# Weight splits on VectorE alone, an earlier register load and regrouped folds in a three-stage fp32 kernel

## The chip, the cores and the metric

The kernel runs on one core of a Trainium2 chip. The metric is the device time of one execution in microseconds (us). Engines are called PE (TensorE), DVE (VectorE), ACT (ScalarE), POOL (GpSimd) and SP (SyncE, which only issues transfers here); PEld is the weight load of TensorE.

## The reference

Three stages are chained: a linear attention with decay over chunks, a mixture of eight experts with one expert for each token, and an FNet block (a Fourier transform over sequence and channels, then a two-layer network). All data are fp32.

```python
# attention: x (4,8,768,32), a (4,8,768), B and C (4,8,768,16), chunks of 32
L = exp(cum[:, None] - cum[None, :]) * causal          # cum: cumulated log a of the chunk
y = (C @ B.T * L) @ x + (C @ state) * exp(cum)
state = exp(sum(la)) * state + B.T @ (x * exp(cum[-1] - cum))
# experts: x (4,768,256), w1 (8,256,1024), w2 (8,1024,256)
fresh = argmax(x @ w_gate)
e = fresh if s == 0 or sigmoid(x @ w_local) < 0.5 else previous token's e
out = p[e] * (relu(x @ w1[e]) @ w2[e])
# FNet
u = x + real(fft(fft(x, axis=1), axis=2))
out = u + relu(layernorm(u) @ w_ch1) @ w_ch2
```

## The kernel before

**Products.** Every fp32 operand of the large products is split into a high part h, rounded to the type fp32r, and a low part l = value - h. One product is then three: hh, hl and lh. The high part of a weight is made by ACT (L180, 128x1024 at a time), the low part by a subtraction of two operands in SBUF (L185): of each 1024 columns VectorE takes the first 384 and GpSimd the other 640. A weight matrix (w1 or w2 of an expert) has two such halves, called q = 0 and 1. SP loads the raw matrices (L160 w1, L164 w2) into a ring of two buffers, which the raw weights of the last network (`rawc`, L115 and L121) share; a buffer is free again when both engines have finished the low part that reads it.

**Stage one** (`phase_a`, from L221): 6 chunks of 128 positions by 2 pairs of batches make 12 passes (`for i, (c, bp) in enumerate(pairs)`). In a pass PE makes small products (g at L414, yb at L445, tl at L498), which are masked by VectorE (mt, L422), and GpSimd prepares operands (ce L338, xt L400, sn L477). Between them a generator, `routing` (from L504), decides the expert of each token by some twenty short VectorE steps for a chunk (mx, kd, ls, cand, ff, er, ot, ac, exo, sx, px, ro, rk, si), interleaved by `gap`, `place` and `leave`. GpSimd then scatters the tokens by row number into xs_buf in HBM (L617). When the last are out, the 256 first tokens of expert 0 are read back (xe, L623). The first expert's split is called from the passes: w1 in passes 8 and 9, the high part of w2 in 9 and 10 and behind them; its low part comes at the start of stage two. `warm` (L262) and `keep_clock` (L213) are products without use that keep PE going.

**Stage two.** `ffn` (L829) runs one expert's tokens: eight column blocks of the first layer (mm1: six products at L839 each, into a ring of three PSUM buffers; then ACT's relu hh, L843, and VectorE's hl, L844), then for each 128 tokens 24 products of the second layer (L851), ACT's y (L900) and GpSimd's scatter into y_tok (L901). Expert 0 comes in two parts, 256 early tokens and 256 others; the seven others run in an order by count (`order`, L793) with 512 tokens for four of them and 384 for the last three. After each mm1 block (0 to 7) and each 128 tokens (8 and on) a hook runs, which sets the order of the rest: the split of the next expert's w1 at hooks 1 and 4, of its w2 at 9 and 10; the tokens of the next expert (xn, loaded by SP at L879) are transposed at hook 7 (tp, L863); `prep_wch` splits pieces of the last network's weights (VectorE L130 to L133, GpSimd L139 and L140). At the end `overflow` (L910) computes on VectorE how many more rounds of experts are needed, loads that number into a register of all five engines (L924) and branches on it (L927); no more are needed with these inputs.

**Stage three** takes z from y_tok (SP, L1026) and runs six groups of 512 rows. For a batch, two `fold` generators (part 0 is a sum, part 1 a difference) make r from z: eo (L1056), tp (L1062), tm (L1065), sp, and r (L1069 to L1074). Two of the six r blocks are on GpSimd (L1069, L1070), and so are eo and tp of part 1 of the first batches. PE transforms r (`stage_a`, L1110, f), corrects and goes on (L1124 and on); VectorE and GpSimd add rows to u (L1157). `run(b, p, n)` takes n steps of fold p of batch b; the order of the opening is written out by hand as such calls.

Of the kernel before, what the change touches and what calls it, by code (L numbers as in the profile page):

```python
# [11 lines left out]
ALU = mybir.AluOpType  # L12
# [5 lines left out]
NE, F = 8, 1024  # L18
# [32 lines left out]
def tile_kernel(ctx: ExitStack, tc: tile.TileContext, io):  # L51
# [103 lines left out]
    def load_w(e, part=None, static=False):  # L155
# [11 lines left out]
        def pieces():  # L167
            out = []
            for k, n, sh in ((0, "w1", [128, 2, F]), (1, "w2", [128, 8, D])):
                r = raws.pop((e, k))  # L170
                hi = wsp.tile(sh, FP32R, tag=n + "h", name=n + "h")
                lo = wsp.tile(sh, FP32R, tag=n + "l", name=n + "l")
                out += [hi, lo]
                h = hi.rearrange("p k f -> p (k f)")
                l_ = lo.rearrange("p k f -> p (k f)")
                r_ = r.rearrange("p k f -> p (k f)")
                ahead = e == 0 and k == 1 and not static

                def high(q):
                    A.activation(out=h[:, q * F:q * F + F], in_=r_[:, q * F:q * F + F], func=ACTF.Copy)  # L180

                def low(q, engs):
                    for eng, x, y in engs:
                        x, y = q * F + x, q * F + y
                        eng.tensor_tensor(out=l_[:, x:y], in0=r_[:, x:y], in1=h[:, x:y], op=ALU.subtract)  # L185

                v, g = (V, 0, 384), (G, 384, F)
                if ahead:
                    for q in range(2):
                        high(q)  # L190
                        yield
                    for eng in (g, v):
                        for q in range(2):
                            low(q, (eng,))
                        if eng is g:
                            yield
                else:
                    for q in range(2):
                        high(q)
                        low(q, (v, g))  # L200
                        if q == 0:
                            yield
                if len(out) == 4:
                    wt[e] = out
                yield
# [15 lines left out]
    def phase_a():  # L221
        with ExitStack() as st:
# [434 lines left out]
            def leave(late=1):  # L657

                if scq and now[0] >= scq[0][2] + late:
                    f, bb, _ = scq.pop(0)  # L660
                    f(bb)
# [28 lines left out]
            for i, (c, bp) in enumerate(pairs):  # L690
# [77 lines left out]
                gap(6)  # L768
                if i in (8, 9, 10):
                    next(ws)  # L770
                    route["ws"] = ws

            g2 = pg.tile([128, 2, 2, 128], FP32, tag="g2", name="g2")[:].rearrange("p u h i -> p (u h i)")
            while rq:
                for r in sorted(rq, key=lambda q: q[2]):
                    if r[1][1]():
                        on = r[1][0]
                        step(r)
                        if on == "p":
                            warm(1, 512, g2)  # L780
                leave(0)
            while scq:
                leave(0)
            next(ws)
            cps = pg.tile([128, 2, 2, 128], FP32, tag="g0", name="cps")[:, 0, 0, 0:NE + 1]
# [123 lines left out]

    def overflow(pools):  # L910

        sm = pools[3]
        ex = sm.tile([128, NE], FP32, tag="oex", name="oex")
        for n in set(CAPS):
# [8 lines left out]
        V.tensor_scalar(out=ri, in0=mx[:, 0:1], scalar1=1.0 / CAP, scalar2=1.499, op0=ALU.mult, op1=ALU.add)  # L923
        nr = nc.values_load(  # L924
            ri[0:1, 0:1], min_val=1, max_val=NTOK // CAP + 1, skip_runtime_bounds_check_because="counts lie in 1..3072"
        )
        with tc.If(nr > 1):  # L927
            ro = sm.tile([128, 4], FP32, tag="oro", name="oro")
# [22 lines left out]
    with ExitStack() as st:  # L951
# [8 lines left out]
        with tc.manual_schedule():  # L960
# [3 lines left out]
            for _ in ws:  # L964
                pass
            nxt, od = None, order(sm)

# [13 lines left out]
            for e in range(NE):  # L981
# [4 lines left out]
                def hook(i):  # L986
                    nonlocal nxt, ws
                    at = (1, 4, 9, 10) if e else (1, 3, 8, 9)
# [13 lines left out]
                wt.pop(e)  # L1002
        overflow((xp, hp, yp, sm, ps1, ps2, pst))
    if "dbg_y" in dbg:
# [4 lines left out]
    with ExitStack() as st:  # L1009
# [35 lines left out]
        def fold(b, part, e1, e2):  # L1045
# [22 lines left out]
            yield  # L1068
            G.tensor_tensor(out=r[:, 3, :], in0=tm[:, 1, :], in1=tm[:, 2, :], op=ALU.add)  # L1069
            G.tensor_tensor(out=r[:, 5, :], in0=tp[:, 1, :], in1=tp[:, 2, :], op=ALU.subtract)  # L1070
            e2.tensor_tensor(out=r[:, 0, :], in0=tp[:, 0, :], in1=sp[:, 0, :], op=ALU.add)
# [161 lines left out]
        with tc.manual_schedule():  # L1233
# [7 lines left out]
            def run(b, p, n=1):  # L1241
                f = fm.get((b, p))
                if f is None:
                    f = fm[b, p] = mid(b) if p == 2 else fold(b, p, G if b > 1 or p else V, V)
                for _ in range(n):
                    next(f)

            run(0, 0)
            run(0, 1)
            run(0, 0, 2)  # L1250
            run(0, 1, 2)
            load_k(0)
            run(1, 0)
            run(1, 1)
            stage_a(0, 0)
# [22 lines left out]
            load_k(1)  # L1278
            run(1, 1)

# [129 lines left out]
```

## Time and profile before

| | us |
|---|---|
| median of 3 runs | 471.1 |
| lowest and highest run | 470.17, 471.72 |
| the profiled execution's own time | 467.85 |
| its span on the core | 466.1 |
| PE busy in the span | 429.4 |
| DVE busy | 272.7 |
| POOL busy | 205.5 |
| ACT busy | 187.1 |

The mean granted clock of PE in the profiled execution is 0.985 of full speed. Busy shares are means over three stages that have different limits. A row of the timeline has the start in us, the duration, the engine, the line, the operation with its output and input, the count, and in brackets how long the engine had been idle and what ended that. The program's names are shared by many instructions, so that mm, say, is the output of L839 and of L851.

### The profile page before, as it was taken

The page shows a single profiled execution, that of the slowest core. Times are in us where ns is not written, and L with a number is a line of the kernel's source. Part 1 is how long each engine was busy: PE and PEld are TensorE (multiplying, and loading weights), DVE is VectorE, ACT ScalarE, POOL GpSimd, SP SyncE. Part 2 cuts the span into 40 slices and gives each one's busy share as a digit, 9 for nine tenths or more (in the row PEclk, how much of TensorE's full clock was granted, in tenths as well). Part 3 has the DMA queues.
Part 4 walks back from the last instruction along what each step waited for, and adds up shares of the span by engine and source line. Part 5 has one row for each costly group of instructions (what it writes and reads, how often), then busy time and mean ns, then how long its engine had stood idle before and what let it go on. Part 6 is the DMA issues. An engine that isn't in the chain of part 4 may idle for free.

```text
span 466.1 us, 8953 instructions
## 1 busy us (share of the span) xinstructions
PE 429.4 (92%) x3429; PEld 370.2 (79%) x3429; DVE 272.7 (59%) x708; ACT 187.1 (40%) x400; POOL 205.5 (44%) x231
## 2 busy tenths in 40 slices
PE   8798788868999899999889879989999999999997
PEld 4576565468989798989879863669989899998986
DVE  5677878584456636464574624786555578564241
ACT  2455463234555445555453411353341443333130
POOL 2237785354437383839493644835302261400000
PEclk9999998999999999999999997999999999999999
DMA  8899411227253645354545116200231100010101
GB/s 277 263 329 350 167 48 49 70 80 242 99 184 124 189 126 186 125 172 133 172 175 169 66 35 227 90 23 1 72 110 51 65 23 25 2 45 1 45 1 45
DMA packets 32891, 54.26 MB, mean 116 GB/s; under 512 B 3301, under 2 KB 22149, under 8 KB 32840
## 3 DMA queue, kind: packets, MB, share of 16 engines
q1 hardware_dynamic: 29400, 45.86, 30.0%
q0 software_dynamic: 2928, 7.46, 4.6%
q8 instruction: 29, 0.48, 0.5%
q10 hardware_dynamic: 512, 0.28, 0.2%
q14 instruction: 22, 0.18, 0.1%
HBM read 41.63 MB, written 12.61 MB: 116 GB/s over the span
## 4 chain that ended last, share of the span: by engine, by line
PE 73%; DVE 12%; DMA 5%; ACT 5%; issue 3%; POOL 1%; SPq 0%; POOLq 0%; ACTq 0%; DVEq 0%
PE mm L851 30%; PE mm L839 26%; DMA xn<-xs_buf 3%; PE tl L498 3%; PE tp L863 2%; PE g L414 2%; PE f L1110 2%; DVE mt L422 2%; PE mb L262 2%; DVE w1l L185 2%; PE yb L445 1%; ACT x1t L452 1%; PE cps L1124 1%; DMA y_tok<-y,ids 1%; DMA z<-y_tok 1%
## 5 line engine op out<-in xcount | busy, mean ns | idle before, releaser
L844 DVE SCALAR_TENSOR_TENSOR hl<-mm,hh 128x512 fp32r<-128x512 f32 (+2 forms) x120 | 74.4, 626 | 59.3 <-ACT hh L843 59.0
L843 ACT ACTIVATE hh<-mm 128x512 fp32r<-128x512 f32 (+2 forms) x120 | 65.1, 547 | 89.1 <-PE mm L839 89.1
L851 PE MATMUL mm<-w2h,hh 128*128 128x256 f32 x232 | 64.9, 280 | 0.0
L851 PE MATMUL mm<-w2l,hh 128*128 128x256 f32 x232 | 64.2, 277 | 0.0
L851 PE MATMUL mm<-w2h,hl 128*128 128x256 f32 x232 | 64.2, 277 | 0.0
L839 PE MATMUL mm<-xh,w1h 128*128 128x512 f32 (+2 forms) x144 | 51.0, 359 | 8.9 <-DVE hl L844 8.3
L851 PE MATMUL mm<-c2h,hh 128*128 128x256 f32 x192 | 54.4, 283 | 0.0
L851 PE MATMUL mm<-c2h,hl 128*128 128x256 f32 x192 | 53.8, 280 | 0.0
L851 PE MATMUL mm<-c2l,hh 128*128 128x256 f32 x192 | 53.7, 280 | 0.0
L901 POOL DMA_INDIRECT y_tok<-y,ids x27 | 28.8, 1068 | 48.7 <-ACT y L900 45.8
L839 PE MATMUL mm<-xh,w1l 128*128 128x512 f32 (+2 forms) x144 | 50.2, 353 | 0.0
L851 PEld LDWEIGHTS mm<-w2h,hl 128*128 128x128 f32 x232 | 43.7, 188 | 0.0
L851 PEld LDWEIGHTS mm<-w2h,hh 128*128 128x128 f32 x232 | 43.6, 188 | 0.0
L851 PEld LDWEIGHTS mm<-w2l,hh 128*128 128x128 f32 x232 | 43.6, 188 | 0.0
L839 PE MATMUL mm<-xh,c1h 128*128 128x512 f32 x96 | 39.5, 411 | 0.6 <-ACT xh L865 0.6
L839 PE MATMUL mm<-xl,w1h 128*128 128x512 f32 (+2 forms) x144 | 39.0, 351 | 0.0
L839 PEld LDWEIGHTS mm<-xh,w1h 128*128 128x128 f32 x144 | 27.6, 192 | 13.2 <-DVE hl L844 10.1
L839 PE MATMUL mm<-xh,c1l 128*128 128x512 f32 x96 | 37.9, 395 | 0.0
L851 PEld LDWEIGHTS mm<-c2l,hh 128*128 128x128 f32 x192 | 36.1, 188 | 0.1
L851 PEld LDWEIGHTS mm<-c2h,hh 128*128 128x128 f32 x192 | 36.1, 188 | 0.1
L851 PEld LDWEIGHTS mm<-c2h,hl 128*128 128x128 f32 x192 | 36.1, 188 | 0.0
L185 POOL TENSOR_TENSOR w1l<-r,w1h 128x640 fp32r<-128x640 f32 x16 | 28.5, 1780 | 15.4 <-ACT w1h L180 15.4
(331 smaller groups left out, 897.2 us busy)
## 6 DMA issues: line engine op xcount, KB each, us to landing
r<-in_w_dram SPq DMA_DIRECT2D x16, 1024.0 KB, 9.3
rawc<-in_wc_dram SPq DMA_DIRECT2D x8, 512.0 KB
out_dram<-o SPq DMA_DIRECT2D x24, 128.0 KB, 1.7
z<-y_tok SPq DMA_DIRECT2D x3, 768.0 KB
xs_buf<-scr SPq DMA_DIRECT2D x8, 265.0 KB, 7.5
xn<-xs_buf SPq DMA_DIRECT2D x4, 530.0 KB, 6.5
c1h<-in_x_dram SPq DMA_DIRECT2D x4, 512.0 KB, 5.6
xk<-y_tok SPq DMA_DIRECT2D x4, 512.0 KB, 3.8
```

The source lines that it names most:

```text
L185: eng.tensor_tensor(out=l_[:, x:y], in0=r_[:, x:y], in1=h[:, x:y], op=ALU.subtract)
L262: PE.matmul(out=ps[:, 0:w], lhsT=wrm[:, 0:128], rhs=wrm[:, 0:w], start=True, stop=True)
L414: PE.matmul(out=gp[q][:, u].rearrange("p h i -> p (h i)"), lhsT=lds[c]["bt"][r:r + 32, 2 * bp + u, :], rhs=ch[r:r + 32, u].rearrange("p q ...
L422: V.tensor_tensor(out=m[:, :, 2 * q:2 * q + 2, :], in0=gp[q], in1=cc("cmask").unsqueeze(1).unsqueeze(1).to_broadcast([128, 2, 2, 128]), op ...
L498: PE.matmul(out=tl[:, 128 * g:128 * g + 137], lhsT=x1t[:, g, u, :], rhs=ca[:, o:o + 137], start=(g == 0), stop=(g == 1), skip_group_check= ...
L839: PE.matmul(out=ps[:, 0:n], lhsT=w[:, d, f * 128:(f + 1) * 128], rhs=x[:, d, 0:n], start=(k == 0), stop=(k == 5))
L843: A.activation(out=hf, in_=ps[:, 0:n], func=ACTF.Relu)
L844: V.scalar_tensor_tensor(out=hl[:, f, 0:n], in0=ps[:, 0:n], scalar=0.0, in1=hf, op0=ALU.max, op1=ALU.subtract)
L851: PE.matmul(out=ps, lhsT=h[:, f, t * 128:(t + 1) * 128], rhs=w[:, f, :], start=(k == 0), stop=(k == 23))
L863: PE.transpose(ps[d][:, t * 128:(t + 1) * 128], src(t, d), ident)
L901: w = G.indirect_dma_start(out=y_tok, out_offset=bass.IndirectOffsetOnAxis(ap=ids[:, t:t + 1], axis=0), in_=y, in_offset=None, bounds_chec ...
L1110: PE.matmul(out=ps[:, k2, :], lhsT=r[:, zi, :], rhs=fa[:, ci, :], start=(i == 0), stop=(i == len(terms) - 1),)
```

## The change

There are three edits.

**Splits.** The low part of every weight is made by VectorE alone, 128x1024 for a half. For the first expert a half is two pieces of 128x512, and the calls come earlier: in passes 7 to 10 one each, in pass 10 a second one; then one behind each product step of the routing's tail, until four more have been taken.

**Rounds.** The number of extra rounds is computed at hook 2 of expert 1 by a generator `rounds` and loaded into the registers at hook 8 of that expert; `overflow` takes the register and only branches.

**Folds.** Of batch 0 all steps of both folds are on VectorE, part 0 ahead of part 1. The first step of the second fold of batch 1 (GpSimd, eo 128x768) moves from ahead of `stage_a(0, 0)` to behind `load_k(1)`.

```diff
-                v, g = (V, 0, 384), (G, 384, F)
-                if ahead:
+                if ahead and k:
                     for q in range(2):
                         high(q)
                         yield
-                    for eng in (g, v):
-                        for q in range(2):
-                            low(q, (eng,))
-                        if eng is g:
-                            yield
-                else:
-                    for q in range(2):
+                for q in range(2):
+                    if not (ahead and k):
                         high(q)
-                        low(q, (v, g))
-                        if q == 0:
-                            yield
+                    if ahead:
+                        low(q * F, q * F + F // 2)
+                        yield
+                        low(q * F + F // 2, q * F + F)
+                    else:
+                        low(q * F, q * F + F)
+                    if q == 0:
+                        yield
...
-                if i in (8, 9, 10):
+                if 7 <= i < NP - 1:
                     next(ws)
+                    if i == 10:
+                        next(ws)
...
                         if on == "p":
                             warm(1, 512, g2)
+                            if low[0] < 4:
+                                next(ws)
+                                low[0] += 1
...
+                    if (e, i) == (1, 2):
+                        nr = rounds(sm)
+                        next(nr)
+                    if (e, i) == (1, 8):
+                        nr = next(nr)
...
-            G.tensor_tensor(out=r[:, 3, :], in0=tm[:, 1, :], in1=tm[:, 2, :], op=ALU.add)
-            G.tensor_tensor(out=r[:, 5, :], in0=tp[:, 1, :], in1=tp[:, 2, :], op=ALU.subtract)
+            e3 = G if b else V
+            e3.tensor_tensor(out=r[:, 3, :], in0=tm[:, 1, :], in1=tm[:, 2, :], op=ALU.add)
+            e3.tensor_tensor(out=r[:, 5, :], in0=tp[:, 1, :], in1=tp[:, 2, :], op=ALU.subtract)
...
-                    f = fm[b, p] = mid(b) if p == 2 else fold(b, p, G if b > 1 or p else V, V)
+                    f = fm[b, p] = mid(b) if p == 2 else fold(b, p, G if b > 1 or b and p else V, V)
...
-            run(0, 0)
-            run(0, 1)
-            run(0, 0, 2)
-            run(0, 1, 2)
+            run(0, 0, 3)
+            run(0, 1, 3)
             load_k(0)
             run(1, 0)
-            run(1, 1)
             stage_a(0, 0)
...
             load_k(1)
-            run(1, 1)
+            run(1, 1, 2)
```

What stood on VectorE in the routing's tail, where exo to si are the last steps ahead of the scatters of the last tokens:

```order
L587 TENSOR_TENSOR exo<-ex,ot 128x16
L591 TENSOR_REDUCE sx<-ex 128x2
L551 SCALAR_TENSOR_TENSOR er<-kr 2x128
L593 TENSOR_SCALAR sx<-sx 128x2
L595 RECIPROCAL sx<-sx 128x2
L567 TENSOR_TENSOR ot<-cb,f__1417 128x2x8
```

The same place in the changed kernel, where L183 is the low part:

```order
L584 TENSOR_TENSOR exo<-ex,ot 128x16
L183 TENSOR_TENSOR w2l<-r_914,w2h 128x512 x2
L588 TENSOR_REDUCE sx<-ex 128x2
L548 SCALAR_TENSOR_TENSOR er<-kr 2x128
L590 TENSOR_SCALAR sx<-sx 128x2
L183 TENSOR_TENSOR w2l<-r_914,w2h 128x512
L592 RECIPROCAL sx<-sx 128x2
L564 TENSOR_TENSOR ot<-cb,f__1419 128x2x8
```

Three pieces of w2's low part now stand between steps of the routing; a fourth follows some rows later. Before, they came after the whole tail.

GpSimd in the middle of stage two, from one 512-token expert to the next:

```order
L185 TENSOR_TENSOR w1l<-r_2595,w1h 128x640 x2
L901 DMA y_tok<-y,ids 3072x256
L139 TENSOR_TENSOR ce__2762<-cv,c1h 128x512
L140 TENSOR_TENSOR c1l<-ce__2762,cr 128x512
L901 DMA y_tok<-y,ids 3072x256
L185 TENSOR_TENSOR w2l<-r_2597,w2h 128x640
L901 DMA y_tok<-y,ids 3072x256
```

And now, where L906 is the scatter:

```order
L906 DMA y_tok<-y,ids 3072x256 x4
L139 TENSOR_TENSOR ce__2518<-cv,c1h 128x512
L140 TENSOR_TENSOR c1l<-ce__2518,cr 128x512
L906 DMA y_tok<-y,ids 3072x256 x4
L139 TENSOR_TENSOR ce__2761<-cv,c1h 128x512
```

Scatters and the two steps of `prep_wch` are left; four subtractions an expert went to VectorE.

GpSimd at the opening of stage three, from the folds of batch 0 to the first rows u:

```order
L1062 TENSOR_TENSOR tp__5527<-eo 128x384
L1069 TENSOR_TENSOR r_5517<-tm__5520 128x128
L1070 TENSOR_TENSOR r_5517<-tp__5519 128x128
L1069 TENSOR_TENSOR r_5525<-tm__5528 128x128
L1070 TENSOR_TENSOR r_5525<-tp__5527 128x128
L1039 DMA xk<-y_tok,rix 128x256 x2
L1056 TENSOR_TENSOR eo<-z 128x768
L1157 TENSOR_TENSOR u<-xk,a 128x256
```

And now, where L1053 loads xk, L1172 makes u and L1070 is eo:

```order
L1053 DMA xk<-y_tok,rix 128x256 x2
L1172 TENSOR_TENSOR u<-xk,a 128x256
L1173 TENSOR_TENSOR u<-xk,a 128x1
L1172 TENSOR_TENSOR u<-xk,a 128x256
L1173 TENSOR_TENSOR u<-xk,a 128x1
L1172 TENSOR_TENSOR u<-xk,a 128x256
L1173 TENSOR_TENSOR u<-xk,a 128x1
L1084 TENSOR_TENSOR r_5495<-tm__5498 128x128
L1085 TENSOR_TENSOR r_5495<-tp__5497 128x128
...
L1053 DMA xk<-y_tok,rix 128x256 x2
L1070 TENSOR_TENSOR eo<-z 128x768
```

The rows u are the first thing that GpSimd does in the stage; eo of batch 1's second fold comes behind the second xk.

## Rows read from the trace of the kernel before

**Rows 1.** From the page: busy time by engine; the chain that ended last.

```profile
PE 429.4 (92%) x3429; PEld 370.2 (79%) x3429; DVE 272.7 (59%) x708; ACT 187.1 (40%) x400; POOL 205.5 (44%) x231
...
PE 73%; DVE 12%; DMA 5%; ACT 5%; issue 3%; POOL 1%; SPq 0%; POOLq 0%; ACTq 0%; DVEq 0%
```

**Rows 2.** Timeline of PE, rows behind a wait: start, us, what, [idle before <-releaser].

```profile
70.47 1.38 PE L414 MATMUL g<-ch,c2h 32*128 32x256 f32 x4 [0.91 <-DVE mt L422]
72.02 2.52 PE L414 MATMUL g<-ch,c2h 32*128 32x256 f32 x12 [0.17 <-DVE mt L422]
...
101.62 0.39 PE L839 MATMUL mm<-xh,w1h 128*128 128x256 f32 x1 [3.28 <-DVE hl L844]
...
115.28 0.39 PE L839 MATMUL mm<-xh,w1h 128*128 128x256 f32 x1 [1.65 <-DVE hl L844]
...
159.79 1.07 PE L863 MATMUL tp<-ca,xn 128*128 128x128 f32 x8 [1.78 <-DMA xn<-xs_buf]
...
226.68 0.85 PE L863 MATMUL tp<-ca,xn 128*128 128x128 f32 x6 [1.43 <-DMA xn<-xs_buf]
...
243.37 0.63 PE L839 MATMUL mm<-xh,w1h 128*128 128x384 f32 x1 [2.05 <-DVE hl L844]
...
264.81 0.44 PE L839 MATMUL mm<-xh,w1h 128*128 128x384 f32 x1 [1.30 <-DVE hl L844]
...
279.08 2.93 PE L213 MATMUL wps<-fa 128*128 128x512 f32 x3 [3.44 <-ACTq L927]
...
294.18 1.16 PE L1110 MATMUL f<-fa,r 128*128 128x128 f32 x8 [0.89 <-POOL r L1069]
...
305.62 0.51 PE L839 MATMUL mm<-xh,c1h 128*128 128x512 f32 x1 [0.58 <-ACT xh L865]
```

**Rows 3.** Timeline of DVE: short mask steps, low parts, and the first fold.

```profile
33.40 0.21 DVE L587 TENSOR_TENSOR exo<-ex,ot 128x32 f32<-128x32 f32 x1
...
66.00 0.56 DVE L185 TENSOR_TENSOR w1l<-r,w1h 128x384 fp32r<-128x384 f32 x1 [1.42 <-ACT w1h L180]
66.48 3.33 DVE L587 TENSOR_TENSOR exo<-ex,ot 128x32 f32<-128x32 f32 x1
...
97.46 3.77 DVE L812 TENSOR_TENSOR bg<-at,cb 128x49 f32<-128x49 f32 x1
...
145.93 2.59 DVE L185 TENSOR_TENSOR w2l<-r,w2h 128x384 fp32r<-128x384 f32 x1 [1.75 <-ACT w2h L180]
...
239.30 3.55 DVE L185 TENSOR_TENSOR w1l<-r,w1h 128x384 fp32r<-128x384 f32 x1
...
286.42 0.56 DVE L1056 TENSOR_TENSOR eo<-z 128x384 f32<-128x384 f32 x1 [0.78 <-DMA z<-y_tok]
```

**Rows 4.** Timeline of POOL at the same places.

```profile
66.62 1.57 POOL L185 TENSOR_TENSOR w1l<-r,w1h 128x640 fp32r<-128x640 f32 x1
...
98.10 1.57 POOL L185 TENSOR_TENSOR w2l<-r,w2h 128x640 fp32r<-128x640 f32 x1
...
149.41 1.59 POOL L185 TENSOR_TENSOR w2l<-r,w2h 128x640 fp32r<-128x640 f32 x1
...
240.86 1.57 POOL L185 TENSOR_TENSOR w1l<-r,w1h 128x640 fp32r<-128x640 f32 x1
...
297.35 1.83 POOL L1056 TENSOR_TENSOR eo<-z 128x768 f32<-128x768 f32 x1
```

**Rows 5.** Chain of waits: two transfers of tokens, from their issue (start, us, what).

```profile
151.63 8.03 DMA xn<-xs_buf
...
220.25 6.30 DMA xn<-xs_buf
```

**Rows 6.** Two stretches: us, busy us of PE, PEld, DVE, ACT, POOL; PEclk; DMA; GB/s.

```profile
70.00:82.00 12.00, 10.16 (x112) 6.51 (x112) 9.72 (x40) 4.48 (x11) 6.04 (x7) 0.86 0.13 47
243.00:247.00 4.00, 3.63 (x12) 3.63 (x13) 2.40 (x5) 0.49 (x1) 1.42 (x1) 0.57 1.03 348
```

**Rows 7.** Source L924, the register load on POOL: ns min/median/max, first and last start.

```profile
L924 POOLq TENSOR_LOAD <-ori x1: 497/497/497, 276.3 to 276.3; - x1
```

More of the change, by code (lines that the diff above doesn't have):

```diff
@@ L176, in pieces, with low @@
                 r_ = r.rearrange("p k f -> p (k f)")
-                ahead = e == 0 and k == 1 and not static
+                ahead = e == 0 and not static
                 def high(q):
                     A.activation(out=h[:, q * F:q * F + F], in_=r_[:, q * F:q * F + F], func=ACTF.Copy)
[L182 to L185, printed above, removed]
-                v, g = (V, 0, 384), (G, 384, F)
-                if ahead:
+                def low(x, y):
+                    V.tensor_tensor(out=l_[:, x:y], in0=r_[:, x:y], in1=h[:, x:y], op=ALU.subtract)
+                if ahead and k:
                     for q in range(2):
@@ L768, in phase_a @@
                 gap(6)
-                if i in (8, 9, 10):
+                if 7 <= i < NP - 1:
                     next(ws)
+                    if i == 10:
+                        next(ws)
                     route["ws"] = ws
+            low = [0]
             g2 = pg.tile([128, 2, 2, 128], FP32, tag="g2", name="g2")[:].rearrange("p u h i -> p (u h i)")
@@ L783, in phase_a @@
                 leave(0)
-            next(ws)
+            while low[0] < 4:
+                next(ws)
+                low[0] += 1
             cps = pg.tile([128, 2, 2, 128], FP32, tag="g0", name="cps")[:, 0, 0, 0:NE + 1]
@@ L908, in moe_expert, with rounds @@
         ffn((hp, ps1, ps2), e, xs, evac, hook, n)
-    def overflow(pools):
-        sm = pools[3]
+    def rounds(sm):
         ex = sm.tile([128, NE], FP32, tag="oex", name="oex")
@@ L923, in overflow @@
         V.tensor_scalar(out=ri, in0=mx[:, 0:1], scalar1=1.0 / CAP, scalar2=1.499, op0=ALU.mult, op1=ALU.add)
-        nr = nc.values_load(
+        yield
+        yield nc.values_load(
             ri[0:1, 0:1], min_val=1, max_val=NTOK // CAP + 1, skip_runtime_bounds_check_because="counts lie in 1..3072"
         )
+    def overflow(pools, nr):
+        sm = pools[3]
         with tc.If(nr > 1):
@@ L965, in tile_kernel @@
                 pass
-            nxt, od = None, order(sm)
+            nxt, nr, od = None, None, order(sm)
             def first(i):
@@ L986, in hook @@
                 def hook(i):
-                    nonlocal nxt, ws
+                    nonlocal nxt, ws, nr
+                    if (e, i) == (1, 2):
[3 more added lines that the diff above has]
+                        nr = next(nr)
                     at = (1, 4, 9, 10) if e else (1, 3, 8, 9)
@@ L1002, in tile_kernel @@
                 wt.pop(e)
-        overflow((xp, hp, yp, sm, ps1, ps2, pst))
+        overflow((xp, hp, yp, sm, ps1, ps2, pst), nr)
     if "dbg_y" in dbg:
```

## The prediction, made before the changed kernel ran

> **What bounds the kernel now.** I read the page first. TensorE is busy for 429.4 of 466.1 us and holds 73% of the chain; VectorE holds 12%, transfers 5% [rows 1]. So the time is PE's work plus the places where PE is made to wait, and a change that adds no product can only win or lose at those places. The next view is therefore PE's timeline, and in it the rows that carry a wait [rows 2]. In stage two they wait for hl of VectorE (3.28, 1.65, 2.05, 1.30) and for the token load xn (1.78, 1.43); in stage one for mt of VectorE; at the start of stage three for r of GpSimd. From 305.62 on I found no wait of 0.2 us or more, so nothing can be won behind that.
>
> The third view, VectorE's timeline at those places, shows why hl and mt are late. The mask step exo takes 0.21 as a rule; at 66.48 it takes 3.33, and bg, a step of nearly that size, takes 3.77 at 97.46 [rows 3]. A low part of 128x384 takes 0.56 when undisturbed and 2.59 and 3.55 elsewhere [rows 3]. Each of these lies beside a GpSimd subtraction of 1.57 to 1.60 us: the step of 66.48 beside that of 66.62, that of 97.46 beside that of 98.10, and the one of 239.30, which ends at 242.85, covers that of 240.86 to 242.43 [rows 3, 4]. All of these VectorE steps read two operands from SBUF. I conclude that such a step is held while GpSimd works through its own two-operand steps, one behind the other.
>
> The Trainium skill (SBUF — State Buffer, section "SBUF: two separate sides") says that VectorE and GpSimd share a pair of ports that one instruction holds to its end, among others for a VectorE step with two inputs in SBUF. By it a VectorE step loses at most one GpSimd step, 1.57 here; the trace shows 3.33 and 3.77, so the holding goes on over several. Were one step the limit, the first two terms below would each fall by some 1.5 us and the time would be about 458.2; the rows decide, and I keep the larger figure.
>
> The fourth view is the clock. PE's mean granted clock is 0.86 over 70 to 82 and 0.57 over 243 to 247, just behind two of the waits [rows 6]. The second is near the lower of its two levels, 1.2 of 2.4 GHz. A long wait therefore costs its own length and then 12 x 0.14 = 1.7 us, or 4 x 0.43 = 1.7 us, of slower products.
>
> **Prices.** From 128x32 in 0.21 and 128x384 in 0.56 [rows 3] the slope is 0.35 us for 352 columns, 1.0 ns a column. A piece of 128x512 is then 0.69 us, a half of 128x1024 is 1.20, an estimate beyond the largest shape seen. Beside the 0.56 that VectorE already spends on a half this adds 0.64 for each of 28 halves (seven experts), 18 us in all. It stands in no row yet. VectorE has 193 us free [rows 1], so it doesn't become the bound as a whole; where a half comes ahead of an hl, the ring of three PSUM buffers gives PE two blocks of cover, and only in the short experts (256 or 384 tokens) is that cover thin.
>
> **The terms, part by part.**
>
> 1. *Stage one.* The stall at 66.48 goes, 3.33 - 0.21 = 3.1, and so do the 1.7 us of clock: 4.8. Against it, VectorE now does four pieces (2.8) in passes 7 to 10 for two of 0.56, and four more (2.8) between the steps of the routing's tail, ahead of the last si and so of the last scatters and the early tokens that stage two begins with. The tail's steps wait in part for PE and ACT anyway; I put half of its 2.8 on the path, and nothing for the passes, where the w1 pieces stand beside PE's products. If that cover is gone, up to 1.7 more is lost there. **-3.4**, from -1.5 to -4.5.
> 2. *Start of stage two.* bg stalls for 3.77 - 0.21 = 3.6, and PE's wait behind it is 3.28 [rows 2, 3]. GpSimd's two w2 steps that cause it are gone from there, and two low parts of VectorE as well. What is late next is xn of expert 0, which is loaded only when the last scatters have landed. **-3.3**, from -2.2 to -3.6.
> 3. *Expert 0's second part.* PE waits 1.65 at 115.28 [rows 2] for an hl behind low parts. They are no longer held by GpSimd but are 1.20 each, in blocks of 256 tokens. I take half, rounded up: **-0.9**, from 0 to -1.65.
> 4. *Token loads.* SP issues its queue in order, and there the raw w2 load (L164), which waits for a buffer that GpSimd's low part still reads, stands ahead of xn. GpSimd's half ended at 149.41 + 1.59 = 151.00 and xn was issued at 151.63 [rows 4, 5]. VectorE began its half at 145.93 [rows 3]; alone it would end at 147.1, 3.9 us earlier, more than the 1.78 that PE waited. The load at 220.25 shows the same with 6.30 us of landing, and PE waited 1.43 [rows 2, 5]. **-3.2**, from -1.8 (the second one still late) to -3.2.
> 5. *The expert before the last.* The wait of 2.05 at 243.37 and the half clock behind it, 1.7, go: 3.8. But its 384 tokens give the next xn less time, and with 6.3 to 8.0 us of landing it will be late by about 1: **-2.8**, from -1.0 to -3.8.
> 6. *The last expert.* PE waits 1.30 at 264.81 for an hl behind the weight pieces of the last network; a GpSimd half is gone beside them, GpSimd's two steps of `prep_wch` stay. Half: **-0.6**, from 0 to -1.3.
> 7. *Rounds.* The load takes 0.50 on POOL [rows 7] behind the last scatters, and PE's wait of 3.44 at 279.08 [rows 2] contains the branch, which stays. Part of the 0.5 goes: **-0.3**, from 0 to -0.5. The moved load stands on all five queues at hook 8 of expert 1, behind some eight short VectorE steps of 0.2 at hook 2. In a 512-token expert these have six blocks of products to hide under; PE queues far enough ahead that its own 0.5 costs nothing. Without that cover it would cost about 0.5.
> 8. *Folds.* The wait of 0.89 for r of GpSimd [rows 2] and GpSimd's eo of 1.83 ahead of the rows u [rows 4] go: 2.7. VectorE gets part 1 on top. From 286.42 on, each part is four steps of 128x384 and eight of 128x128; with 0.48 from start to start (66.00 to 66.48) and 0.2 each, both end at 286.42 + 2 x 3.5 = 293.4, ahead of the 294.18 of PE's present start, though by the full durations (0.56, 0.21) it would be level. GpSimd's eo now lies behind the second xk load, so r of batch 1 comes late and PE waits there instead, in the first group. Half: **-1.4**, from 0 to -2.7.
>
> Sum: 3.4 + 3.3 + 0.9 + 3.2 + 2.8 + 0.6 + 0.3 + 1.4 = 15.9. The profiled execution of 467.85 would come to 452.0. It is 3.25 below the median of the runs, 471.1, which is what counts: 471.1 - 15.9 = **455.2 us**. The small ends add up to 6.5 (464.6), the large ends to 21.3 (449.8).
>
> **The rivals.**
>
> *Half of it comes back as new waits.* VectorE's longer low parts and pieces stand ahead of hl and the routing. Then terms 1, 2, 4, 5 and 7 give 1.5, 3.3, 3.2, 1.0 and 0.3, the others nothing: 9.3, or 461.8. For it speaks that the low part grows from 384 to 1024 columns in the short experts too, where PE has least cover; against it that VectorE is idle 41% of the span [rows 1] and the worst stalls are longer than any step that is added.
>
> *Scatters are held.* Now VectorE has the long two-operand steps, and GpSimd's scatters stand beside them. Four pieces of 0.69 in the tail would then delay the last scatters by up to 2.8 and not 1.4, and a scatter beside one of the last expert's halves by up to 1.2: 455.2 + 2.6 = 457.8. No row here shows a scatter that was held so long. The box on SWDGE in the same section of the Trainium skill's page says that a transfer issued by GpSimd can starve while VectorE has the ports; this is the rule that speaks against the change.
>
> *Slower.* In stage two VectorE's hl becomes what PE follows, because each half goes ahead of an hl in VectorE's order. If all of the 0.64 that a half gains reaches PE, 28 x 0.64 = 17.9 is lost, two more than the 15.9 that the other terms give: 473.1. It decides from 15.9 / 28 = 0.57 a half. Against it: in the 512-token experts, from 159.79 to 226.68, [rows 2] has waits for xn and none for hl, with the cover of three buffers.
>
> *Not what it says.* If the stalls come from any GpSimd step (sn and xt of stage one remain, and `prep_wch`), terms 1, 3, 5 and 6 vanish: 15.9 - 7.7 = 8.2, or 462.9.
>
> **How the numbers follow.** Forecast 0.54; half comes back 0.20; scatters held 0.08; not what it says 0.07; slower 0.08; and 0.03 for a change that ends level, all gains met by new waits. The first four are faster, so 0.89, 0.03 and 0.08. A difference under 0.3% (1.4 us) can't be told from no change. The range from 450.0 to 464.5 leaves out the level and slower cases and a little at either end, and is as wide as the ends of the sum.
>
> **What would show it.** In the changed profile exo near 66 and bg near 97 should take 0.2, the clock over the last passes should stay near 1.0, low parts should take 1.2 with no long tail, and PE's rows should have no wait over 0.5 for hl. xn should be issued within 1 us of VectorE's second w2 half. In the tail, si should come some 3 us earlier. GpSimd's busy time should fall by about 50 (32 steps of 1.57), VectorE's rise by 5 to 15: 18 for the halves and some for expert 0 and the folds, less the stalls. The prediction is wrong if stalls of over 2 us stay on VectorE with GpSimd's subtractions gone, or if PE waits for hl in every short expert.

## The result

The changed kernel takes 455.0 us (median of 4 runs, 453.65 to 457.3) where the kernel before takes 470.85 (4 runs, 470.17 to 471.72): a ratio of 0.966, 95% interval 0.962 to 0.970. The forecast was 455.2 with a range of 450.0 to 464.5. The profiled execution of the changed kernel, however, is its slowest one, 457.3 us (span 455.5), while that of before was faster than the median. So the two traces differ by 10.6 us of span, and the medians by 15.9. One reason is that TensorE runs at half clock for some stretches of an execution, and that where and for how long differs between executions of one kernel; so the traces below are read by stretches.

The page of the changed kernel, busy time by engine:

```profile
PE 429.5 (94%) x3429; PEld 370.3 (81%) x3429; DVE 275.9 (61%) x719; ACT 187.0 (41%) x400; POOL 148.4 (33%) x192
```

GpSimd loses 57 us, VectorE gains only 3 although its 28 later halves alone are some 18 us more work: what it got in work it got back in stalls. In its timeline (start, us, what) the steps of [rows 3] are short now:

```profile
65.58 0.20 DVE L584 TENSOR_TENSOR exo<-ex,ot 128x32 f32<-128x32 f32 x1
...
66.99 1.19 DVE L590 TENSOR_SCALAR sx<-sx 128x4 f32<-128x4 f32 x1
...
97.44 0.21 DVE L817 TENSOR_TENSOR bg<-at,cb 128x49 f32<-128x49 f32 x1
...
138.90 2.27 DVE L183 TENSOR_TENSOR w2l<-r,w2h 128x1024 fp32r<-128x1024 f32 x1 [1.65 <-ACT w2h L180]
```

exo went from 3.33 to 0.20 and bg from 3.77 to 0.21. Smaller stalls stay. The low part of 138.90 takes 1.05 more than the usual 1.23, and the first w2 half of the three experts behind it takes 1.34 to 1.63; beside each stands the two-operand step of `prep_wch` that stayed on GpSimd. The step sx, which reads one operand and takes 0.15 in the kernel before, takes 1.19 beside sn and xt of stage one; no row of TensorE waits for VectorE there. GpSimd's timeline at both places, with the scatters behind the second:

```profile
67.11 0.47 POOL L474 TENSOR_TENSOR sn<-st,sn 128x128 f32<-128x128 f32 x1
67.52 1.19 POOL L397 TENSOR_TENSOR xt<-c1l,f_sb 128x256 f32<-128x256 f32 x2
...
138.77 1.32 POOL L140 TENSOR_TENSOR c1l<-ce__2028,cr 128x512 fp32r<-128x512 f32 x1
140.24 1.81 POOL L906 DMA_INDIRECT y_tok<-y,ids  x1
142.35 1.35 POOL L906 DMA_INDIRECT y_tok<-y,ids  x1 [0.30 <-issue]
144.00 0.97 POOL L906 DMA_INDIRECT y_tok<-y,ids  x1 [0.30 <-issue]
```

TensorE's rows that still carry a wait of more than 0.6 us in stages two and three, against [rows 2]:

```profile
111.00 0.39 PE L844 MATMUL mm<-xh,w1h 128*128 128x256 f32 x1 [0.92 <-DVE hl L849]
...
238.28 0.85 PE L868 MATMUL tp<-ca,xn 128*128 128x128 f32 x6 [0.97 <-DMA xn<-xs_buf]
...
300.39 0.80 PE L1125 MATMUL f<-fa,r 128*128 128x128 f32 x4 [0.97 <-DVE r L1086]
```

Beside these there are a wait at the branch (2.98, before 3.44) and one of 0.94 for r at 282.65 (1.79 in the second trace). The waits of 3.28 and 2.05 for hl and of 1.78 and 1.43 for xn are gone. SP shows why for xn: the raw load and xn leave at 142.88 and 143.48, right behind VectorE's half, which starts at 141.63 and takes 1.23; before, xn left at 151.63 [rows 5].

```profile
142.88 0.37 SPq L164 DMA_DIRECT2D r<-in_w_dram  x1
143.48 0.39 SPq L884 DMA_DIRECT2D xn<-xs_buf  x1
```

Stretch by stretch, from the start of a named row of TensorE, GpSimd or VectorE to that of the next (us; "again" is a second trace of the changed kernel, from the experiments):

| stretch | before | after | again | forecast | measured |
|---|---|---|---|---|---|
| to g of the tenth pass | 58.10 | 58.32 | 60.77 | 0 | +0.2 |
| to tp of the early tokens (term 1) | 35.22 | 34.99 | 31.17 | -3.4 | -0.2 (-4.0) |
| to tp of expert 0's second part (2) | 13.38 | 9.85 | 9.87 | -3.3 | -3.5 |
| to tp of expert 1 (3) | 11.23 | 10.45 | 10.58 | -0.9 | -0.8 |
| to tp of expert 6 (4) | 108.75 | 105.63 | 105.64 | -3.2 | -3.1 |
| to tp of expert 7 (5) | 21.49 | 19.04 | 18.78 | -2.8 | -2.5 |
| to the last scatter (6) | 28.31 | 28.06 | 27.73 | -0.6 | -0.3 |
| to the first eo of VectorE (7) | 8.60 | 9.20 | 8.64 | -0.3 | +0.6 (0.0) |
| to tp of the second group (8) | 46.27 | 45.10 | 45.10 | -1.4 | -1.2 |

Terms 2 to 8 were forecast at -12.5 and measured at -10.7 (-11.7 in the second trace). Term 1 is the odd one: in the first trace of the changed kernel almost nothing of it is left.

### The profile page after: what moved, and what is told of

It reads as the page before. It is cut to its first block, busy times and chain, and to the rows that moved or that the text cites. A ratio compares the mean times of both kernels' runs of the same rounds, so it can differ in the third digit from the quotient of the medians.

```text
span 455.5 us, 8893 instructions
## 1 busy us (share of the span) xinstructions
PE 429.5 (94%) x3429; PEld 370.3 (81%) x3429; DVE 275.9 (61%) x719; ACT 187.0 (41%) x400; POOL 148.4 (33%) x192
## 5 line engine op out<-in xcount | busy, mean ns | idle before, releaser
L906 POOL DMA_INDIRECT y_tok<-y,ids x27 | 33.7, 1249 | 98.9 <-ACT y L905 78.2
L844 PE MATMUL mm<-xh,w1h 128*128 128x512 f32 (+2 forms) x144 | 50.1, 353 | 2.2 <-DVE hl L849 1.6
L844 PE MATMUL mm<-xh,w1l 128*128 128x512 f32 (+2 forms) x144 | 49.4, 348 | 0.0
L844 PE MATMUL mm<-xh,c1h 128*128 128x512 f32 x96 | 39.4, 411 | 0.6 <-ACT xh L870 0.6
L844 PE MATMUL mm<-xl,w1h 128*128 128x512 f32 (+2 forms) x144 | 38.6, 348 | 0.0
L183 DVE TENSOR_TENSOR w2l<-r,w2h 128x1024 fp32r<-128x1024 f32 (+1 forms) x18 | 21.5, 1199 | 27.7 <-ACT w2h L180 27.7
L844 PE MATMUL mm<-xh,c1l 128*128 128x512 f32 x96 | 37.9, 395 | 0.0
L419 DVE TENSOR_TENSOR mt<-g,ca 128x512 f32<-128x512 f32 x48 | 31.4, 677 | 5.1 <-PE g L411 4.9
```

What stands on the lines that cost most here:

```text
L183: V.tensor_tensor(out=l_[:, x:y], in0=r_[:, x:y], in1=h[:, x:y], op=ALU.subtract)
L419: V.tensor_tensor(out=m[:, :, 2 * q:2 * q + 2, :], in0=gp[q], in1=cc("cmask").unsqueeze(1).unsqueeze(1).to_broadcast([128, 2, 2, 128]), op ...
L844: PE.matmul(out=ps[:, 0:n], lhsT=w[:, d, f * 128:(f + 1) * 128], rhs=x[:, d, 0:n], start=(k == 0), stop=(k == 5))
L906: w = G.indirect_dma_start(out=y_tok, out_offset=bass.IndirectOffsetOnAxis(ap=ids[:, t:t + 1], axis=0), in_=y, in_offset=None, bounds_chec ...
```

## The experiments

Each run was compared with the kernel before on its own chip. The runs of the first two groups of four had it at 470.42 and 471.51, those of the last four at 481.75, on a chip on which stage one takes some 10 us longer; those four are read against each other and by stretches.

**The changed kernel and the kernel before, again (after_again, before_again).** No edit.

> The changed kernel as it is, run again. In its first profile the end of stage one ran at a granted clock of 0.50 from 80 to 90 us, and stage two began at 93.31 us, where it began before (93.32), though the last pass was 4.4 us ahead. Theory A (that half clock is an accident of the profiled execution): most executions have a mean clock of 0.992 or more and take 453.5 to 455.5 us, and a profile without the half clock begins stage two at 89 to 90 us. Theory B (the half clock is the rule and the early splits bring nothing): most executions show 0.981 and 457 us.

> The kernel of before run again, for a second trace of it. Its first profiled execution took 467.85 us, the timed ones 470.2 to 471.7. Theory A (the clock at the end of stage one falls in some executions of before, too): a profile of 470 to 472 us has a stretch of half clock between 82 and 96 us that the first does not have, and starts stage two some 3 us later. Theory B (the difference lies elsewhere): stage two starts at 93.3 us again.

The changed kernel took 454.83 (6 runs, 453.64 to 456.68), its profile 454.81 at a mean clock of 0.992. The kernel before took 469.42 (8 runs, 468.06 to 475.2), and the traced execution is the slowest of them, 475.2, at a mean clock of 0.964. It shows how far an execution can go, not how often. Two views tell the story: the granted clock by stretches (us; PE busy; PEclk; DMA; GB/s), of the changed kernel's first trace, of its second, and of the second trace of before:

```profile
75.00:80.00 5.00, 3.24 (x45) 1.00 0.15 55
80.00:85.00 5.00, 4.98 (x15) 0.51 0.25 92
85.00:90.00 5.00, 5.00 (x10) 0.50 0.24 71
```

```profile
75.00:80.00 5.00, 4.12 (x62) 1.00 0.29 106
80.00:85.00 5.00, 3.64 (x21) 1.00 0.15 55
85.00:90.00 5.00, 4.39 (x18) 1.00 0.24 69
```

```profile
75.00:80.00 5.00, 4.74 (x47) 0.53 0.09 32
80.00:85.00 5.00, 5.00 (x45) 0.50 0.22 81
85.00:90.00 5.00, 4.57 (x39) 0.50 0.15 54
90.00:95.00 5.00, 5.00 (x13) 0.50 0.32 99
```

And the first product of stage two in the same order, after, after again, before again:

```profile
93.31 0.60 PE L868 MATMUL tp<-ca,xe 128*128 128x128 f32 x4
```

```profile
91.94 0.60 PE L868 MATMUL tp<-ca,xe 128*128 128x128 f32 x4
```

```profile
102.11 0.60 PE L863 MATMUL tp<-ca,xe 128*128 128x128 f32 x4
```

The first trace of the changed kernel has half clock for some 10 us from 80 on; its products in the routing's tail take twice as long, and the 4.4 us that the passes had won are spent there. The second trace has no such stretch and the tail's stretch is 31.17 us, 4.0 less than before's 35.22. (Its 91.94 contains 2.4 us of a later start of the passes, which lies ahead of every part of the change.) Three traces further down have the same stage one as the changed kernel, and half clock at the same place, from 80.5 to 81.0 on for 3.4 to 6.8 us (`low_twice`, `folds_back`, `eo_first`, a line each):

```profile
80.00:85.00 5.00, 4.61 (x15) 0.59 0.22 81
80.00:85.00 5.00, 4.77 (x16) 0.66 0.22 81
80.00:85.00 5.00, 4.54 (x15) 0.60 0.22 81
```

There the stretch of term 1 takes 33.32, 32.19 and 33.30. So of five traces of this stage one, four lose something to the clock, and term 1 gives 0.2, 1.9, 3.0, 1.9 and 4.0 against the first trace of before.

The kernel before can have it in a worse form: in its second trace exo stalls as in the first, half clock lasts from 75 to 99 us, and the stretch takes 41.38. The step bg, however, is not held there:

```profile
69.11 3.32 DVE L587 TENSOR_TENSOR exo<-ex,ot 128x32 f32<-128x32 f32 x1
...
107.61 0.21 DVE L812 TENSOR_TENSOR bg<-at,cb 128x49 f32<-128x49 f32 x1
```

GpSimd's two w2 steps had ended at 105.35, before bg began, and the next stretch takes 11.19 and not 13.38. So 2.2 of the 6.2 us that the tail lost come back in term 2's stretch. Theory A holds for both kernels in that the clock differs between executions, but its size was off for the one before: 102.11 is 8.8 us later than 93.32, where I expected 3; 2.6 of them lie ahead of the tenth pass and 6.2 in the stretch. In both traces of before, and in that of `first_back` below, the clock falls some 6 us behind the start of the stalled exo; the change removes that stall. How much of the 15.9 us between the medians this makes is not shown.

**The first expert's split as before (first_back).**

```diff
-                if 7 <= i < NP - 1:
+                if i in (8, 9, 10):
                     next(ws)
...
-                        low(q * F, q * F + F)
+                        low(q, (v, g) if both else ((V, 0, F),))
...
```

(`low` takes engines again, `both` is expert 0, and the calls in the routing's tail go.)

> Only the first expert's split is as it was before: low parts on both engines, in passes 8 and 9 and at the start of stage two. My theory puts terms 1 and 2 of the sum here (3.4 and 3.3 us), so 455.0 + 6.7 = 461.7 us, with exo near 66 us and bg near 97 us stalled for over 3 us again. Rival (the clock takes what the early pieces give): only the 3.5 us of bg come back, 458.5 us.

463.42 (6 runs, 459.69 to 468.6), 8.6 above the changed kernel in the same group. Its VectorE timeline:

```profile
69.55 3.33 DVE L588 TENSOR_TENSOR exo<-ex,ot 128x32 f32<-128x32 f32 x1
...
100.57 3.77 DVE L813 TENSOR_TENSOR bg<-at,cb 128x49 f32<-128x49 f32 x1
```

```profile
104.72 0.39 PE L840 MATMUL mm<-xh,w1h 128*128 128x256 f32 x1 [3.27 <-DVE hl L845]
```

Both stalls are back to a hundredth of a microsecond, PE waits 3.27 for hl at 104.72 as in [rows 2], half clock lasts 3.4 us from 75.8 on as it did in before from 72.8, and the two stretches take 35.26 and 13.38, as before the change. Terms 1 and 2 were forecast at 6.7; by the stretches they are 4.1 + 3.5 = 7.6 against the second trace, where the clock holds. The rival's 458.5 is out.

**Two products without use in the last pass (tail_warm).**

```diff
                 rows(i, 0)
                 if more:
                     carry(i + 1)
+                else:
+                    g2 = pg.tile([128, 2, 2, 128], FP32, tag="g2", name="g2")[:].rearrange("p u h i -> p (u h i)")
+                    warm(1, 512, g2)
                 place()
                 place()
+                if not more:
+                    warm(1, 512, g2)
                 rows(i, 1)
...
-            g2 = pg.tile([128, 2, 2, 128], FP32, tag="g2", name="g2")[:].rearrange("p u h i -> p (u h i)")
```

> The changed kernel with one more product without use behind each of the two idle places of PE in the last pass (79 and 80 us), so that PE goes on into the routing's tail. Theory A (PE's idle time at 78 to 80 us lets the clock fall): no execution has the half clock at 80 to 90 us, the slow ones among the timed go, and the median is 453.5 to 454.5 us. Rival (the fall comes by chance or from elsewhere, and the fillers are in the way): the spread stays as it is, 453.6 to 457.3 us, or the time rises by up to 1 us.

453.89 (6 runs, 453.29 to 456.93) against 454.83. Its profile keeps the clock at 1.00 from 80 to 90 us, but two of the six runs are above 456, as one of the changed kernel's was. Four of the five traces without these products have half clock there, but one trace with them is too little to call it rarer, and the median is not clearly better. This one is left open.

**GpSimd with one operand, in the kernel before (one_input).**

```diff
-                        eng.tensor_tensor(out=l_[:, x:y], in0=r_[:, x:y], in1=h[:, x:y], op=ALU.subtract)
+                        if eng is G:
+                            G.tensor_scalar(out=l_[:, x:y], in0=h[:, x:y], scalar1=0.0, scalar2=None, op0=ALU.mult)
+                        else:
+                            eng.tensor_tensor(out=l_[:, x:y], in0=r_[:, x:y], in1=h[:, x:y], op=ALU.subtract)
```

> The kernel of before, with GpSimd's share of each low part as a step that reads one operand (h times zero) and not two; the low part of those columns is zero, so that part of the precision is left out. Theory A (a GpSimd step holds two-operand steps of VectorE whenever it reads SBUF): exo near 66 to 69 us and the low parts of VectorE are held as before, by at least the 1 to 1.6 us of a GpSimd step, and the time stays within 2 us of 470. Theory B (only steps of two operands on both engines hold each other): exo takes 0.2 us, the low parts 0.56, and the time falls to 456 to 460 us.

458.04 (4 runs, 456.0 to 460.64) against 471.51: 13.5 us less, with not one column moved. The low parts by line (ns min/median/max, first and last start), VectorE's and then GpSimd's:

```profile
L188 DVE TENSOR_TENSOR w1l<-r,w1h x16: 552/559/560, 66.6 to 232.2; 128x384 fp32r<-128x384 f32 x16
L188 DVE TENSOR_TENSOR w2l<-r,w2h x16: 548/559/1026, 93.0 to 246.0; 128x384 fp32r<-128x384 f32 x16
```

```profile
L186 POOL TENSOR_SCALAR w1l<-w1h x16: 1800/2170/2232, 67.2 to 233.1; 128x640 fp32r<-128x640 f32 x16
```

GpSimd's steps became longer, 1.8 to 2.2 us, and lie beside VectorE's as before, but no low part of w1 takes over 0.56, where the kernel before had 3.55. So the long stalls of VectorE come from GpSimd steps of two operands. Four low parts of w2 still take 0.97 to 1.03, beside the two-operand steps of `prep_wch`. And exo, beside a GpSimd step of one operand, takes 0.99 there and not 0.2:

```profile
67.04 0.99 DVE L590 TENSOR_TENSOR exo<-ex,ot 128x32 f32<-128x32 f32 x1
```

Theory B is right on the time and on the long stalls, but its "only" is too strong: beside a GpSimd step of one operand VectorE can lose time too, less than 1 us here. The stretches of terms 1, 2, 3 and 5 take 32.72, 10.01, 9.43 and 18.91, where before has 35.22, 13.38, 11.23 and 21.49. That of term 4 takes 105.42 for 108.75, but there a second cause can't be told apart: GpSimd's step no longer reads the raw weights either, so their buffer comes free without it.

**Every later low part twice (low_twice).**

```diff
-                    V.tensor_tensor(out=l_[:, x:y], in0=r_[:, x:y], in1=h[:, x:y], op=ALU.subtract)
+                    for _ in range(1 if e == 0 or static else 2):
+                        V.tensor_tensor(out=l_[:, x:y], in0=r_[:, x:y], in1=h[:, x:y], op=ALU.subtract)
```

> The changed kernel with every low part of experts 1 to 7 made twice, so that VectorE has 28 x 1.2 = 34 us more of the work that the change put there. It measures the price of the rival by which the longer halves reach PE. Theory (they are covered but for the short experts): 2 to 8 us more, 457 to 463 us, with the waits for hl in the experts of 384 and 256 tokens and late token loads. Rival (hl is what PE follows): each 1.2 us reaches PE, 34 us more, 489 us.

471.74 (10 runs, 467.76 to 474.37), about 17 more than the changed kernel. I expected 2 to 8, and the rival 34: both miss. From the early tokens to the branch it is 188.97 against 174.49, 14.5 us or 0.52 for each of the 28 halves. Up to 3.4 us of it, an estimate, are clock: behind the first wait for hl the granted clock is 0.67 from 110 to 115 and 0.65 from 115 to 120, 5 x 0.33 + 5 x 0.35 = 3.4 us lost, and the second trace of the changed kernel has no such stretch there. Without that it is 0.40 for each half. PE's timeline shows it in every expert, one row each of 256, 512 and 384 tokens:

```profile
110.96 0.39 PE L845 MATMUL mm<-xh,w1h 128*128 128x256 f32 x1 [2.17 <-DVE hl L850]
...
155.40 0.50 PE L845 MATMUL mm<-xh,w1h 128*128 128x512 f32 x1 [0.68 <-DVE hl L850]
...
225.32 0.44 PE L845 MATMUL mm<-xh,w1h 128*128 128x384 f32 x1 [1.40 <-DVE hl L850]
```

The change stands just ahead of that edge. In `one_input` VectorE has halves of 0.56, in the changed kernel of 1.23, and the 512-token experts take 22.69 in both; only expert 0's second part is 1.1 us and one later expert 0.4 us longer. The next 1.2 us of a half cost 1.0 us in each 512-token expert and 1.3 to 2.0 in those of 384. The price of the halves isn't a line but an edge, and the slower rival was closer than its chance of 0.08 says.

**xn ahead of the raw w2 load, in the kernel before (xn_first).**

```diff
                     xn = load_x(pools, e + 1)
+                    if e:
+                        ws = load_w(e + 1, 1)
...
-                            ws = load_w(e + 2) if e + 2 < NE else None
+                            ws = load_w(e + 2, 0) if e + 2 < NE else None
```

> The kernel of before with one edit in SP's order: the next expert's tokens (xn) are loaded ahead of the raw w2 matrix and not behind it. Theory (term 4: xn was late because it stood behind a load that waited for GpSimd's low part): the waits of 1.78 and 1.43 us for xn go, xn is issued within 1 us of the end of an expert, and the part from the third to the sixth expert's transposes takes 3.2 us less. Rival (xn is late because its buffer or the transfer itself is late): the waits stay.

477.66 (12 runs) against 481.75, a ratio of 0.994 (0.989 to 1.000), hardly clear of no change; the rows say more. No row of PE waits for xn any more: the expert of 24.62 us takes 22.69 and the one of 21.49 takes 19.89, together 3.5 less. Of that 1.1 is lost again in the next, whose stretch grows from 21.49 to 22.63 behind two waits for hl (1.00 and 2.02). Term 4's cause, SP's order behind a load that waits for GpSimd, is shown; moving VectorE's half and moving the load are two cures for it.

**The folds as before (folds_back).**

```diff
-            run(0, 0, 3)
-            run(0, 1, 3)
+            run(0, 0)
+            run(0, 1)
+            run(0, 0, 2)
+            run(0, 1, 2)
...
             run(1, 0)
+            run(1, 1)
             stage_a(0, 0)
...
-            run(1, 1, 2)
+            run(1, 1)
```

(with the engines of the folds as they were)

> Only the folds are as before. By my sum they give 1.4 us: 456.4 us. By the profile of the changed kernel the first group starts 1.6 us earlier against the end of stage two and all of it is given back in that group: 455.0 us, no difference from the end of stage two to the second group's start.

455.91 (4 runs, 454.58 to 456.98). The stretch of term 8 takes 46.18, as before the change (46.27), against 45.10 in both traces of the changed kernel: the folds give 1.1 us. What the changed kernel wins ahead of the first group (up to 2.6) it gives back in that group, which takes 27.2 from its first product (L844) against 25.7, but only in part. My expectation that all of it is given back was wrong, the forecast of 1.4 nearly right.

**Batch 1's eo ahead of the second xk load (eo_first).**

```diff
+            run(1, 1)
             load_k(1)
-            run(1, 1, 2)
+            run(1, 1)
```

> The changed kernel with the first step of batch 1's second fold (GpSimd, eo 128x768) ahead of the second load of xk and not behind it. In the changed kernel xk's two issues and eo end at 296.9 us and PE waits 0.97 for r at 300.39. Theory (the gain of the folds is given back because that eo comes too late): the wait goes, and from the start of the first group's products to the end of that group it takes 0.8 to 1.5 us less than in the changed kernel; 453.5 to 454.2 us. Rival (the queue of GpSimd as a whole is the limit, xk then comes late instead): no difference in that stretch.

455.28 (4 runs, 452.32 to 459.64), no gain that can be seen; its profile has half clock from 279 to 293, so the stretch can't be read in it. The last run below (`best_b`) has the same edit at full clock there and shows what happens. On VectorE and on GpSimd:

```profile
300.84 1.90 DVE L1096 SCALAR_TENSOR_TENSOR r<-sp,tm__5511 128x128 f32<-128x128 f32 x1
```

```profile
300.72 1.88 POOL L1078 TENSOR_TENSOR eo<-z 128x768 f32<-128x768 f32 x1
```

There eo falls beside VectorE's last fold steps; one that takes 0.28 alone takes 1.90, xl behind it is late, and PE waits 0.79 for xl instead of 0.97 for r. The stretch of term 8 takes 44.88 there, 0.2 less than in the changed kernel, where I expected 0.8 to 1.5. The hold that the change removes in two stages comes back in the third.

**The rounds as before (rounds_back).**

```diff
-                    if (e, i) == (1, 2):
-                        nr = rounds(sm)
-                        next(nr)
-                    if (e, i) == (1, 8):
-                        nr = next(nr)
...
+        nr = rounds(sm)
+        next(nr)
+        nr = next(nr)
         overflow((xp, hp, yp, sm, ps1, ps2, pst), nr)
```

> Only the rounds are as before: computed and loaded at the end of stage two on all engines. By my sum that edit gives 0.3 us (0 to 0.5). Theory: 455.1 us, and from the last scatter's issue on GpSimd to the first transfer of z it takes 0.5 us more than in the changed kernel. Rival (the load is hidden behind the branch of other engines): that stretch and the time stay.

465.11 (6 runs, 463.26 to 467.95), 0.970 of its own before, where the changed kernel has 0.966 and 0.970. From the last scatter to SP's transfer of z it takes 4.97 us, in the traces of the changed kernel 5.63 and 5.05. So the rival was right: moving the rounds away from there, POOL's load of 0.50 with them, wins nothing that can be seen.

**Edits together (best_a, best_b).** The first has the edits of `tail_warm`, `eo_first` and `xn_first` on the changed kernel, the second also this:

```diff
+        with tc.manual_schedule():
+            keep_clock(ps1, 7)
         overflow((xp, hp, yp, sm, ps1, ps2, pst), nr)
```

> The changed kernel with three edits: the two products without use in the last pass, batch 1's eo ahead of the second xk load, and xn ahead of the raw w2 load. If the stretches add up, 0.97 (xn) and 1.5 us (eo) go, and the half clock in the routing's tail is rarer: 451.5 to 452.5 us. Rival (PE's clock falls elsewhere in their place): 453.5 to 455 us, with a wider spread.

> The same with seven products without use on PE ahead of the branch at the end of stage two, where PE waits 3 us. Theory (the idle time there is what lets the clock fall in the opening of stage three): clock near 1.0 from there to the first group and 451 to 452 us with a narrow spread. Rival (the products hold up PE's branch, or the clock falls later in real work): no gain over the kernel without them, up to 1 us more.

469.02 (6 runs, 464.56 to 470.17) and 465.35 (463.86 to 466.55), beside 465.11 for the changed kernel with the rounds as before. The expert before last gets shorter, 17.91 us against 18.78 to 19.04, so xn's wait is gone, but in the first trace half clock lasts from 54 to 68, from 88 to 95 and from 307 to 310. With the seven products at the branch the clock stays at 1.00 from 260 to 300. Both forecasts, 451.5 to 452.5 and 451 to 452, were of a gain of some 3 us, and none is seen: no version here beats the changed kernel clearly.

## Why the prediction was right, and where it was not

The time is right, and most of the sum is right term by term; that it agrees to 0.2 us is partly luck, as the two profiled executions differ by 5 us less.

Term 1 (-3.4): right in the trace where the clock holds (-4.0), 0.2 to 3.0 in the four where it falls. The step that failed is the treatment of the clock. I counted the half clock of before, 1.7 us, as the price of that one stall and let it vanish with it. It is not a fixed price: behind the same stall of exo a second trace of before took 6.2 us more in that stretch than the first, and the changed kernel, without the stall, had 3 to 10 us of half clock there in four traces and none in the fifth. The 1.7 in term 5 is no fixed price either: the second trace of before has the wait of 2.02 and no half clock behind it. Of the pieces in the tail I put half on the path, 1.4 us. Without half clock they cost some 0.5: from the last tl of the tail to the early tokens it is 9.48 (82.46 to 91.94 in the second trace) against 8.94 before (84.38 to 93.32).

Term 2 (-3.3), 3 (-0.9), 4 (-3.2) and 5 (-2.8): -3.5, -0.8, -3.1 and -2.5. In term 4 the second load gave 1.2, not 1.43, since a longer half delays an hl there: L183 of 214.26 takes 1.22, hl behind it ends at 215.95, and PE's next product starts at 216.01. In term 5 the forecast loss of 1 for the next xn is the 0.97 at 238.28. The conclusion under them, that VectorE's two-operand steps are held by GpSimd's, is what `one_input` shows for the long stalls; it is not the whole, as sx is held with one operand (1.19 at 66.99) and exo takes 0.99 beside a one-operand step.

Term 6 (-0.6): -0.3, or -0.6 in the second trace. The 1.30 at 264.81 became 0.31.

Term 7 (-0.3): 0. The step that failed is putting POOL's register load on the path. In the trace of before that load ends at 276.83, and y_tok's last scatter lands at 279.35; only then does GpSimd go on, and z leaves at 281.79. So the load ran beside the scatter.

Term 8 (-1.4): -1.2, 2.6 won ahead of the first group and 1.5 given back in it. Which wait would be next, f of batch 1 for r behind the late eo, came as forecast, at 0.97.

The rivals. Half of it comes back (461.8): out by the time; its new waits are there, but small (0.92 at 111.00, 0.97 at 238.28). Scatters are held: they are (1.81 and 1.35 behind 140.24 against 0.97), but in stage two, where no row of PE waits for them; in the tail they take 0.97 to 1.08, 1.18 once in the second trace. Slower was priced by a straight line of 0.64 a half. Measured, the first 0.64 costs near nothing and the next 1.2 costs 0.52, 0.40 without the clock. Not what it says (462.9): sn and xt of stage one do hold sx, but exo and bg at 0.20 and 0.21 show that the long stalls went with the subtractions.

The Trainium skill (SBUF — State Buffer, section "SBUF: two separate sides") has the shared ports held by one instruction to its end, by which exo would have lost at most the one GpSimd step beside it, 1.57. exo lost 3.1, in both traces of before and again in `first_back`; here the trace differs and the larger figure was the right one.

What stays open: why the clock falls in one execution and not in the next at the same place, and how often the kernel before runs as in its slower trace. How much of the gain goes with the clock can be estimated from the mean clock of each run, on the chip of the first four runs. There the medians are 470.07 (25 runs of before, mean clock 0.978) and 454.83 (6 of the changed kernel, 0.992), 15.2 apart. The four runs of each that lie between 0.988 and 0.992 have medians of 467.0 and 454.9, 12.1 apart. So some 12 us go with the work and the waits and some 3 with the clock; that the removed stall is what keeps the clock up is not shown.

## What to carry to other kernels

When VectorE has a short step of three microseconds, look at what GpSimd runs beside it; if both have two operands in SBUF, giving GpSimd's share back to VectorE can cost VectorE next to nothing (3 us of busy time here). Compare stretches between fixed rows and not only spans, and take a second trace before a clock stretch is booked as a gain. Before more is put ahead of what TensorE waits for, double it once: the edge of the cover shows in one run.

## What the runs showed of the hardware

- A two-operand step of VectorE in SBUF is held through several two-operand steps of GpSimd in a row: 3.33 and 3.32 us for a step of 0.21 in two traces of one kernel, 3.33 again in another. Beside one-operand GpSimd steps of 1.8 to 2.2 us, VectorE's 16 low parts of w1 took 0.552 to 0.560, but one step of 0.2 took 0.99.
- A step of VectorE with one operand can be held too: sx, 0.15 in the kernel before, took 1.19 beside two-operand GpSimd steps (0.47 and twice 0.6).
- GpSimd's scatters beside VectorE's 1.23 us halves take up to 1.99 us, where they take 0.97 alone.
- One kernel's TensorE began stage two at 93.32 in one execution and at 102.11 in another, with the same order and the same stall of exo; behind that stall half clock lasted 3.4 us in the first and 23.9 in the second.
